# GpSimd as second choice for two kinds of low parts, w_in in four tensors, and the planner's new numbers

## The chip, the cores and the metric

The kernel runs on one core of a Trainium2 chip. The time is the device time of that core in microseconds (us). The engines are TensorE (PE in the profile; its weight loads PEld), VectorE (DVE), ScalarE (ACT), GpSimd (POOL) and SyncE (SP), whose queue issues nearly all DMAs. Three executions of the kernel before took 720.46, 721.92 and 986.96 us, median 721.92.

## The reference

Eight sequences b of 576 tokens go through an attention with 32 packed queries, twice, and then through a feed-forward layer with a gate:

```python
s = scale * q @ k.T ; a = exp(s - max) / (sum + 1e-9) ; sm_attn = a @ v
p_packed = sm_attn(p, k, v)             # 8 heads, 32 x 64 each
x = sm_attn(q, p_packed, p_packed)      # 576 x 512 for each b
h = x @ w_in                            # 512 -> 2048
g = h * erf(softplus(h))
out = g @ w_out                         # 2048 -> 512
```

w_in and w_out come as 64-bit floats. The kernel converts them to 32 bits itself, by a scaled copy on ACT and three bit operations on DVE.

## The kernel before, in words

Every product of the feed-forward layer is made from two 32-bit halves: a value is rounded to a high part (`hi`, type fp32r), the low part is the value minus that (`lo`), and PE multiplies hi by hi, lo by hi and hi by lo. So each tensor that PE reads there exists twice: `a2h` and `a2l` (the second attention's probabilities of a b), `wph` and `wpl` (w_in's block j multiplied into that b's packed values, "w prime"), `gh` and `gl` (the gated h), `woh` and `wol` (a tile of w_out).

The work is cut into units (b, f): f is one of 16 column tiles of 128 of the hidden 2048. `h_unit` makes h for one unit in two chunks of 288 tokens, six matmuls of 128x288 each, into two PSUM banks tagged `ps_h`, from which ACT copies them to `hs`. `gate_group` takes up to four units: ACT does softplus and erf (two tables, loaded each time), DVE multiplies (`hs<-t,hs`), rounds (`gh<-hs`) and subtracts (`gl<-hs,gh`). `o_unit` multiplies four token blocks by w_out's tile, three matmuls of 128x512 each, and adds them up in four PSUM banks. The 64 tokens of a b that are left over go through a DRAM tensor `rest` and are done for pairs of b (`o_rest`, matmuls `or`).

`load_w_in` and `load_w_out` bring a weight tile by DMA to a staging buffer (`wi`, `wos`), and `convert` turns it into 32 bits: ACT copy, DVE shift (`TENSOR_SCALAR`), and two DVE `SCALAR_TENSOR_TENSOR` that merge in the sign and the low word. w_out's tile is then rounded to `woh` (ACT or DVE) and `wol` is subtracted on DVE. The first block of w_in is loaded in two pairs (`load_w_in_pair`), staged in the room that blocks 2 and 3 take later.

What runs when is set by a list scheduler inside the kernel. Each operation is an `Op` with an engine, a key (its place in line, from the table `PLAN`), a cost in us and its dependencies. `Program.order` plays the program through with these costs: whenever an engine is free, it takes the ready operation with the lowest key whose buffers have room. The instructions are emitted in the order of the starts that come out, and each engine then runs its own in exactly that order. An operation may have a second engine (`also`): it stands in that engine's line too, with its key raised by a number from `PLAN["also"]`, and whichever of the two gets to it first has it.

Before the first h, PE waits for the first b's attention; `warm` transposes fill that time. Lines of the profile: L292 all matmuls, L297 to L301 the conversion, L346 wol, L457 the exponentials of the first two b, L549 and L550 a2h and a2l, L571 and L572 wph and wpl in one piece, L576 and L577 in two, L588 softplus, L593 erf, L598, L600 and L602 the gate's multiply, gh and gl, L624 the copy of h.

Of the kernel before, what the change touches and what calls it, by code (L numbers as in the profile page):

```python
# [43 lines left out]
    "first conv": (-9.39, 1.51),  # L44
    "whole k": 1,
}
# [24 lines left out]
class Program:  # L71
# [34 lines left out]
    def order(self):  # L106
# [14 lines left out]
        came = {op: 0.0 for op in self.ops}  # L121
# [11 lines left out]
        while events:  # L133
# [15 lines left out]
            for engine, line in ready.items():  # L149
# [3 lines left out]
                for i, (_, _, op) in enumerate(line):  # L153
# [10 lines left out]
                    break  # L164
                if pick is None:
                    continue
                op = line.pop(pick)[2]
# [21 lines left out]
                if engine in ("SP", "POOL") or op.kind == "dma":  # L189
                    state["bus"] = max(state["bus"], now + busy + self.SEND[0]) + op.dur / self.SEND[1]  # L190
                    end = state["bus"] + self.SEND[2] + PLAN["late"]
                else:
                    end = now + busy + op.dur
                count += 1
# [12 lines left out]
def act_us(n):  # L207
    return 0.05 + 0.00088 * n

# [6 lines left out]
def tile_pack_attention_moe(ctx: ExitStack, tc: tile.TileContext, qT, kT, v, pT, w_in, w_out, out, rest):  # L216
# [65 lines left out]
    def dma(key, size, emit, w, r, engine="SP", after=()):  # L282
        return prog.add(engine, key, 0.45 if engine != "POOL" else 1.0, size, lambda: line(engine, emit()), w, r,
                        kind="dma" if engine == "ACT" else 0, after=after)

    ident = fixed([P, P], "ident")
    w_in_sb = fixed([P, 4, DFF], "w_in_sb")
# [6 lines left out]
    def convert(key, dst, of, low, high, n, w, r):  # L294
# [3 lines left out]
        dve(key, n, lambda: nc.vector.tensor_scalar(bits(), bits(), 3, None, op0=ALU.logical_shift_left), w, (), True)  # L298
# [22 lines left out]
    def load_w_in_pair(sent, key, c):  # L321
        w = ((w_in_sb, (c, 0)), (w_in_sb, (c + 1, 0)))
        dst = lambda: w_in_sb[:, c:c + 2, 0:FB]
        src = w_in[c * P:(c + 2) * P, 0:FB].rearrange("(c p) n -> p c n", p=P)
        if w_in.dtype == F32:
            dma(sent, 2 * P * FB * 4, lambda: nc.sync.dma_start(dst(), src), w, ())
            return
        there = tuple((w_in_sb, (c + i, j)) for i in range(2) for j in (2, 3))
        raw = lambda: w_in_sb[:, c:c + 2, 2 * FB:4 * FB]
        dma(sent, 2 * P * FB * 8, lambda: nc.sync.dma_start(raw().bitcast(I64), src), there, ())  # L330
# [3 lines left out]
        convert(key, dst, None, words(0), words(1), 2 * FB, w, there)  # L334

    def load_w_in(sent, key, j, c):
        load_f32(sent, key, lambda: w_in_sb[:, c, j * FB:(j + 1) * FB], ((w_in_sb, (c, j)),),
                 w_in[c * P:(c + 1) * P, j * FB:(j + 1) * FB], f"wi{j}_{c}")

    def load_w_out(sent, key, f):  # L340
# [5 lines left out]
        dve(key, DM, lambda: nc.vector.tensor_tensor(lo[:], made[:], hi[:], op=ALU.subtract), (lo,), (made, hi))  # L346
# [3 lines left out]
    settled = []  # L350
# [11 lines left out]
    def products(key, names, wheres, left, rights, r, after=()):  # L362
# [12 lines left out]
        return places  # L375

    def attention(b, keys):
# [52 lines left out]
        if first:  # L430
# [4 lines left out]
                          [[pb] + [half(k, c, x) for c in range(NC)] for x in range(2)], () if roomy else settled[-1:])  # L435
# [78 lines left out]
        pt[b] = ptt  # L514
        ta, tb = big("ta", [P, 2, S]), big("tb", [P, 2, S])
        hi, lo = buf("a2h", [P, 2, S], f"a2h{b}", F32R), buf("a2l", [P, 2, S], f"a2l{b}", F32R)
        nb = 2 * HT // NK
        both = buf("mx", [P, 2 * nb], f"mx{b}")
# [35 lines left out]

    def w_prime(key, *pieces):
# [5 lines left out]

        def emit(b, j, hi, lo, banks, w, whole):
            return [mm(banks[r]()[NK * c:NK * c + NK, :], pt[b][64 * r:64 * r + 64, NK * c:NK * c + NK],
                       w_in_sb[64 * r:64 * r + 64, c, j * FB:(j + 1) * FB], start=True, stop=True)
                    for c in range(NC) for r in range(2)]
        pe(key, W_US * len(made), lambda: [i for piece in made for i in emit(*piece)], sum((x[5] for x in made), ()),
           [x for b, j in pieces for x in [pt[b]] + [(w_in_sb, (c, j)) for c in range(NC)]], 1)
        for i, (b, j, hi, lo, banks, w, whole) in reversed(list(enumerate(made))):
# [10 lines left out]
            wp[b, j] = (hi, lo)  # L579

    gs, group, before, sent_rest, heads = {}, [], [[]], {}, []

    def gate_group(e):
# [12 lines left out]
        for t, (hs, b, f, n) in zip(ts, group):  # L596
# [5 lines left out]
            dve(key, S, lambda hs=hs, ghi=ghi, glo=glo: nc.vector.tensor_tensor(glo[:], hs[:], ghi[:], op=ALU.subtract),  # L602
                (glo,), (hs, ghi))
# [6 lines left out]
    def h_unit(n, b, f):  # L610
# [3 lines left out]
        fo = f % PER * P  # L614
        for c in range(2):
            ps = buf("ps_h", [P, 512], f"h{b}_{f}_{c}")
            terms = [(r, w, a) for r in range(2) for w, a in ((whi, ahi), (whi, alo), (wlo, ahi))]
            cols = (lambda a, r, c=c: a[:, c, r * HT:(r + 1) * HT])
            if n == 0:
                terms = terms[0::3] + terms[1::3] + terms[2::3]  # L620
            made = pe(n + c / 2, 0.797, lambda c=c, ps=ps, terms=terms, cols=cols: [
                mm(ps[:, 0:HT], w[:, r, fo:fo + P], cols(a, r), start=(m == 0), stop=(m == 5))
                for m, (r, w, a) in enumerate(terms)], (ps,), (whi, wlo, (ahi, c), (alo, c)))
            op = act(n + c / 2 - PLAN["copy"], HT, lambda c=c, ps=ps: nc.scalar.copy(hs[:, c * HT:(c + 1) * HT], ps[:, 0:HT]),  # L624
                     ((hs, c),), (ps,))
            also("h", op, "DVE", dve_us(HT), lambda c=c, ps=ps: nc.vector.tensor_copy(hs[:, c * HT:(c + 1) * HT], ps[:, 0:HT]))
# [73 lines left out]
    w_prime(-40 + PLAN["wp first"], (0, 0))  # L700
# [87 lines left out]
```

## Time and profile before

| what | value |
|---|---|
| median of three executions | 721.92 us |
| the profiled execution's own time | 722.06 us |
| its span | 720.3 us |
| so outside the span | 1.8 us |
| PE busy | 705.3 us, 98% of the span |
| ACT busy | 495.8 us, 69% |
| DVE busy | 432.6 us, 60% |
| POOL busy | 7.9 us, 1% |
| first h matmul starts | 33.95 us |
| last o matmul starts | 710.92 us |

"Busy" counts the time in which at least one instruction of an engine is under way; overlapping matmuls count once. An idle time has behind it in brackets what ended it. Rows of a timeline give start, duration, engine, line, operation, output and inputs; the durations of consecutive instructions overlap by some 0.08 us on DVE and ACT, so what one more instruction costs is the distance from its start to the next start.

### The profile page before, as it was taken

How to read it: one execution, taken by the hardware profiler on the slowest of the kernel's cores; microseconds unless marked ns; L12 is line 12 of the kernel's file. 1: busy time of each engine (PE TensorE's matmuls, PEld its weight loads, DVE VectorE, ACT ScalarE, POOL GpSimd, SP SyncE). 2: the span in 40 equal slices, each digit the busy share in tenths (PEclk: the TensorE clock that was granted, in tenths of full speed). 3: DMA queues.
4: the chain of work that ended last, by engine and by line, in shares of the span. 5: the costliest groups of instructions: out<-in, count | busy, mean ns of one | idle time of the engine just before them, and what ended most of it. 6: DMA issues, size and time to landing. Idle time of an engine off the chain costs nothing.

```text
span 720.3 us, 13230 instructions
## 1 busy us (share of the span) xinstructions
PE 705.3 (98%) x5159; PEld 576.7 (80%) x5159; DVE 432.6 (60%) x707; ACT 495.8 (69%) x831; POOL 7.9 (1%) x14
## 2 busy tenths in 40 slices
PE   7889999999999999999999999999999999999997
PEld 6657887878878888787888878887878878788885
DVE  3899998898654754566545545467545564354540
ACT  3399999988874576766855758567858555676731
POOL 0000000002001000000000000000000000000000
PEclk9999999999999999999999999999999999999999
DMA  9962485754338300253006220063102210021104
GB/s 321 303 228 65 119 248 148 254 190 75 95 100 183 86 12 17 91 163 101 18 13 216 70 75 15 16 215 97 43 17 87 95 31 16 15 74 45 44 19 132
DMA packets 66399, 74.80 MB, mean 104 GB/s; under 512 B 40224, under 2 KB 42272, under 8 KB 66336
## 3 DMA queue, kind: packets, MB, share of 16 engines
q1 hardware_dynamic: 64816, 71.14, 32.0%
q0 software_dynamic: 1152, 2.10, 2.2%
q8 instruction: 40, 0.66, 0.4%
q10 hardware_dynamic: 368, 0.72, 0.3%
q14 instruction: 23, 0.19, 0.1%
HBM read 54.00 MB, written 19.92 MB: 103 GB/s over the span
## 4 chain that ended last, share of the span: by engine, by line
PE 83%; ACT 11%; DMA 3%; SPq 1%; issue 1%; DVE 0%; ACTq 0%
PE o L292 45%; PE h L292 25%; PE or L292 6%; PE wp L292 4%; PE s L292 2%; ACT L593 1%; ACT t L593 1%; ACT L588 1%; ACT hs L624 1%; ACT t L588 1%; DMA v<-v 1%; PE p L292 1%; DMA q<-qT 1%; DMA wi<-w_in 1%; PE t L477 1%; ACT w_in_sb L297 1%
## 5 line engine op out<-in xcount | busy, mean ns | idle before, releaser
L292 PE MATMUL o<-woh,gh 128*128 128x512 f32 x512 | 205.7, 402 | 0.5 <-DVE gh L600 0.5
L292 PE MATMUL o<-woh,gl 128*128 128x512 f32 x512 | 201.8, 394 | 0.5 <-DVE gl L602 0.5
L292 PE MATMUL o<-wol,gh 128*128 128x512 f32 x512 | 200.8, 392 | 0.0
L624 ACT COPY hs<-h 128x288 f32<-128x288 f32 x256 | 98.9, 395 | 129.9 <-PE h L292 128.9
L292 PE MATMUL h<-a2h,wph 128*128 128x288 f32 x512 | 152.5, 298 | 1.8 <-ACT a2h L549 1.6
L292 PE MATMUL h<-a2h,wpl 128*128 128x288 f32 x512 | 150.4, 294 | 0.7 <-DVE wpl L572 0.7
L292 PE MATMUL h<-a2l,wph 128*128 128x288 f32 x512 | 150.7, 295 | 0.3 <-DVE a2l L550 0.3
L598 DVE TENSOR_TENSOR hs<-t,hs 128x576 f32<-128x576 f32 x128 | 95.2, 753 | 60.0 <-ACT t L593 58.2
L292 PEld LDWEIGHTS o<-woh,gh 128*128 128x128 f32 x512 | 96.1, 188 | 34.1 <-issue 17.9
L292 PEld LDWEIGHTS o<-wol,gh 128*128 128x128 f32 x512 | 96.2, 188 | 22.0
L292 PEld LDWEIGHTS h<-a2h,wph 128*128 128x128 f32 x512 | 96.0, 188 | 14.9 <-ACT hs L624 3.6
L292 PEld LDWEIGHTS o<-woh,gl 128*128 128x128 f32 x512 | 96.2, 188 | 12.5 <-DVE gl L602 0.8
L600 DVE CAST gh<-hs 128x576 fp32r<-128x576 f32 x128 | 58.0, 456 | 77.6 <-PE o L292 76.1
L292 PEld LDWEIGHTS h<-a2l,wph 128*128 128x128 f32 x512 | 96.1, 188 | 8.8 <-DVE a2l L550 0.5
L602 DVE TENSOR_TENSOR gl<-hs,gh 128x576 fp32r<-128x576 f32 x128 | 96.1, 753 | 2.8 <-DMA rest<-gl 0.8
L292 PEld LDWEIGHTS h<-a2h,wpl 128*128 128x128 f32 x512 | 96.1, 188 | 0.9 <-DVE wpl L572 0.9
L588 ACT ACTIVATE t<-hs 128x576 f32<-128x576 f32 x128 | 87.2, 686 | 2.7 <-DVE hs L598 0.2
L593 ACT ACTIVATE t<-t 128x576 f32<-128x576 f32 x128 | 83.6, 685 | 0.4
L588 ACT ACT_TABLE_LOAD x38 | 48.8, 1283 | 0.7
L593 ACT ACT_TABLE_LOAD x38 | 48.8, 1283 | 0.7
L292 PE MATMUL or<-woh,g 128*128 128x512 f32 x128 | 40.2, 395 | 0.0
L654 ACT COPY ob<-o 128x512 f32<-128x512 f32 x40 | 22.8, 587 | 24.8 <-PE o L292 24.7
(98 smaller groups left out, 578.0 us busy)
## 6 DMA issues: line engine op xcount, KB each, us to landing
q<-qT SPq DMA_DIRECT2D x32, 288.0 KB, 4.2
v<-v SPq DMA_DIRECT2D x32, 256.0 KB, 3.8
wos<-w_out SPq DMA_DIRECT2D x16, 512.0 KB, 3.5
out<-ob SPq DMA_DIRECT2D x32, 256.0 KB, 2.8
g<-rest SPq DMA_DIRECT2D x16, 512.0 KB, 3.2
k<-kT SPq DMA_DIRECT2D x26, 288.0 KB, 4.5
wi<-w_in SPq DMA_DIRECT2D x12, 512.0 KB, 4.9
rest<-gh SPq DMA_DIRECT2D x128, 32.0 KB, 1.5
```

Of the source, the lines that this page charges most:

```text
L292: return nc.tensor.matmul(*args, **kw)
L297: act(key, n * 1.06, lambda: nc.scalar.mul(dst(), high().bitcast(F32), F64_SCALE), w, r)
L477: return [nc.tensor.transpose(tbanks[x]()[:, (j % 2 * 2 + r) * P:(j % 2 * 2 + r + 1) * P], a[:, r, j * P:(j + 1) * P], ident[:]) for j in ...
L588: done.append(act(n + PLAN["lag"] - PLAN["act"] - 2, S, lambda t=t, hs=hs: nc.scalar.activation(t[:], hs[:], AF.Softplus), (t,), (hs,), ru ...
L593: erfs.append(act(e + PLAN["lag"] - PLAN["act"] - 4 + i, S, lambda t=t: nc.scalar.activation(t[:], t[:], AF.Erf), (t,), (), run="erf", kin ...
L598: dve(key, S, lambda t=t, hs=hs: nc.vector.tensor_tensor(hs[:], t[:], hs[:], op=ALU.mult), (hs,), (t,))
L600: op = dve(key, S, lambda hs=hs, ghi=ghi: nc.vector.tensor_copy(ghi[:], hs[:]), (ghi,), (hs,), True)
L602: dve(key, S, lambda hs=hs, ghi=ghi, glo=glo: nc.vector.tensor_tensor(glo[:], hs[:], ghi[:], op=ALU.subtract), (glo,), (hs, ghi))
L624: op = act(n + c / 2 - PLAN["copy"], HT, lambda c=c, ps=ps: nc.scalar.copy(hs[:, c * HT:(c + 1) * HT], ps[:, 0:HT]), ((hs, c),), (ps,))
L654: act(key - 1, DM, lambda: nc.scalar.copy(ob[:], to[:]), (ob,), (to,))
```

## The change

**Second choices.** The subtraction that makes `wol` and the one that makes `gl` in the first 24 units (`"low until": 24`) get GpSimd as a second engine, both with nothing added to their key (`'w_out low': 0, 'low': 0`). The planner books `pool_us(n)`, 0.3 + 0.0037 n us, for them. A third possible second choice, the conversion's shift, is written but not in the table.

**w_in in four tensors.** One tensor of 128 x 4 x 2048 becomes four of 128 x 4 x 512, `w_in0` to `w_in3`. The first block's pairs are staged in the whole of `w_in2` and of `w_in3`.

**Other edits.** The first w prime is made by a function of its own, `w_prime_first`, which moves its two PSUM banks out one by one (512 columns each) where one instruction moved both (1024). Options that are switched off come along: `direct` and the branches that need it, `patience` (0), `halves` (1). The key of "packs" changes from 2.35 to 4.61, and "norm", which nothing used, goes.

```diff
-    "also": {'w_out': 10.23, 'turned': 8.26, 'packs': 2.35, 'norm': 0.2},
+    "also": {'w_out': 10.23, 'turned': 8.26, 'packs': 4.61, 'w_out low': 0, 'low': 0},
...
+    "low until": 24,
...
+def pool_us(n):
+    return 0.3 + 0.0037 * n
...
-    w_in_sb = fixed([P, 4, DFF], "w_in_sb")
+    HALVES = PLAN["halves"]
+    FN = FB // HALVES
+    w0 = [fixed([P, NC, FN], f"w_in0{x}") for x in range(HALVES)]
+    wi = [None] + [fixed([P, NC, FB], f"w_in{j}") for j in range(1, NFB)]
...
-        dve(key, DM, lambda: nc.vector.tensor_tensor(lo[:], made[:], hi[:], op=ALU.subtract), (lo,), (made, hi))
+        op = dve(key, DM, lambda: nc.vector.tensor_tensor(lo[:], made[:], hi[:], op=ALU.subtract), (lo,), (made, hi))
+        also("w_out low", op, "POOL", pool_us(DM), lambda: nc.gpsimd.tensor_tensor(lo[:], made[:], hi[:], op=ALU.subtract))
...
+            for r in range(2):
+                act(keys[x], FN, lambda hi=hi, r=r, banks=banks, at=at: nc.scalar.copy(hi[:, r, at], banks[r]()[:, 0:FN]),
+                    ((hi, (x, r)),), (w[r % len(w)],))
...
+            if n < PLAN["low until"]:
+                also("low", op, "POOL", pool_us(S), lambda hs=hs, ghi=ghi, glo=glo: nc.gpsimd.tensor_tensor(
+                    glo[:], hs[:], ghi[:], op=ALU.subtract))
...
-    w_prime(-40 + PLAN["wp first"], (0, 0))
+    w_prime_first([-40 + k for k in PLAN["wp first"]])
```

What the scheduler makes of it is seen in the order of the instructions on each engine. POOL had nothing between its start and its eight output DMAs. It now has 24 subtractions there, six `wol` and 18 `gl`. These are the first of them (in a name such as gl_3_934, 3 is the tile f, and the last number tells instances apart):

```order
L374 TENSOR_TENSOR wol_722<-wo_672,woh_718 128x512
L722 TENSOR_TENSOR gl_1_786<-hs_1_566,gh_1_780 128x576
L374 TENSOR_TENSOR wol_867<-wo_727,woh_852 128x512
L374 TENSOR_TENSOR wol_890<-wo_764,woh_869 128x512
L722 TENSOR_TENSOR gl_3_934<-hs_3_599,gh_3_927 128x576
L722 TENSOR_TENSOR gl_4_998<-hs_4_807,gh_4_986 128x576
L722 TENSOR_TENSOR gl_5_1086<-hs_5_849,gh_5_1074 128x576
L722 TENSOR_TENSOR gl_6_1115<-hs_6_881,gh_6_1112 128x576
L722 TENSOR_TENSOR gl_7_1151<-hs_7_929,gh_7_1141 128x576
```

Eight of these nine stand ahead of the last gate rounding of the first segment (gh_7) or beside it: three wol and five gl, up to gl_6.

On ACT, around the first a2h, before (wi_0 to wi_3 are the four pieces of w_in's second block, a_1 the second b's exponentials, hs the copied h):

```order
L297 ACTIVATE w_in_sb<-wi_0_232 128x512
L297 ACTIVATE w_in_sb<-wi_1_239 128x512
L549 CAST a2h_503<-tb_491 128x576
L297 ACTIVATE w_in_sb<-wi_2_247 128x512
L549 CAST a2h_503<-tb_491 128x576
L457 ACTIVATE a_1_535,ms_441<-s_1_0_0_391,m_522 128x288
L457 ACTIVATE a_1_535,ms_441<-s_1_0_1_393,m_522 128x288
L457 ACTIVATE a_1_535,ms_441<-s_1_1_0_402,m_522 128x288
L457 ACTIVATE a_1_535,ms_441<-s_1_1_1_404,m_522 128x288
```

And there now:

```order
L320 ACTIVATE w_in_84<-wi_0_235 128x512
L320 ACTIVATE w_in_84<-wi_1_242 128x512
L594 CAST a2h_504<-tb_491 128x576
L320 ACTIVATE w_in_84<-wi_2_250 128x512
L320 ACTIVATE w_in_84<-wi_3_257 128x512
L751 COPY hs_0_538<-h_0_0_520 128x288
L499 ACTIVATE a_1_548,ms_440<-s_1_0_0_395,m_512 128x288
L499 ACTIVATE a_1_548,ms_440<-s_1_0_1_397,m_512 128x288
L499 ACTIVATE a_1_548,ms_440<-s_1_1_0_407,m_512 128x288
L499 ACTIVATE a_1_548,ms_440<-s_1_1_1_409,m_512 128x288
L594 CAST a2h_504<-tb_491 128x576
```

The fourth piece wi_3 and a copy of h have moved ahead of the exponentials, and the second a2h behind them.

Further on, on ACT ahead of the second w prime's high part, before:

```order
L588 ACTIVATE t_1_691<-hs_1_553 128x576
L297 ACTIVATE wo_722<-wos_668 128x512
L593 ACT_TABLE_LOAD
L593 ACTIVATE t_1_691<-t_1_691 128x576
L588 ACT_TABLE_LOAD
L588 ACTIVATE t_2_758<-hs_2_645 128x576
L571 CAST wph_1_771<-wp_1_749 128x1024
L297 ACTIVATE wo_774<-wos_715 128x512
```

And there now:

```order
L705 ACTIVATE t_1_694<-hs_1_566 128x576
L320 ACTIVATE wo_727<-wos_661 128x512
L710 ACT_TABLE_LOAD
L710 ACTIVATE t_1_694<-t_1_694 128x576
L320 ACTIVATE wo_764<-wos_716 128x512
L705 ACT_TABLE_LOAD
L705 ACTIVATE t_2_766<-hs_2_574 128x576
L668 CAST wph_1_778<-wp_1_753 128x1024
```

One more conversion of a w_out tile (wo_764) stands ahead of wph_1.

On DVE, between the first gl and the second w prime's low part, before:

```order
L346 TENSOR_TENSOR wol_747<-wo_656,woh_717 128x512
L538 TENSOR_REDUCE mx_760<-ta_726 128x36
L598 TENSOR_TENSOR hs_1_553<-t_1_691,hs_1_553 128x576
L539 TENSOR_TENSOR ta_726<-ta_726,mx_760 128x1152
L572 TENSOR_TENSOR wpl_1_776<-wp_1_749,wph_1_771 128x1024
L600 CAST gh_1_781<-hs_1_553 128x576
L298 TENSOR_SCALAR wo_722<-wo_722 128x512
L602 TENSOR_TENSOR gl_1_792<-hs_1_553,gh_1_781 128x576
```

And there now:

```order
L321 TENSOR_SCALAR wo_727<-wo_727 128x512
L583 TENSOR_REDUCE mx_762<-ta_731 128x36
L715 TENSOR_TENSOR hs_1_566<-t_1_694,hs_1_566 128x576
L584 TENSOR_TENSOR ta_731<-ta_731,mx_762 128x1152
L717 CAST gh_1_780<-hs_1_566 128x576
L669 TENSOR_TENSOR wpl_1_784<-wp_1_753,wph_1_778 128x1024
L323 SCALAR_TENSOR_TENSOR wo_727<-wos_661,wo_727 128x512
```

wol and gl_1 are gone from DVE here, and the shift and gh_1 have moved ahead of wpl_1. PE's instructions are the same in number, and their last 80 rows are in the same order; in the first part of the program h and o blocks have changed places by a few.

More of the change, by code (lines that the diff above doesn't have):

```diff
@@ L120, in order @@
         state = {"table": None, "within": False, "kind": 0, "bus": 0.0}
-        came = {op: 0.0 for op in self.ops}
+        unsent, due = {op: len(op.deps) for op in self.ops}, {op: 0.0 for op in self.ops}
+        soon = {e: [] for e in ready}
+        patience, until = PLAN["patience"]
         events, count = [(0.0, 0, None)], 0
@@ L164, in order @@
                     break
+                soon[engine] = [(t, op) for t, op in soon[engine] if waits[op]]
                 if pick is None:
                     continue
-                op = line.pop(pick)[2]
+                op = line[pick][2]
+                if now < until and any(op2.key < op.key - 2 and t - now < patience and now + op.busy > t + 0.05
+                                       for t, op2 in soon[engine]):
+                    continue
+                line.pop(pick)
                 if op.other:
@@ L188, in order @@
                 free[engine] = now + busy
[L189 removed]
+                if op.kind == "dma":
                     state["bus"] = max(state["bus"], now + busy + self.SEND[0]) + op.dur / self.SEND[1]
@@ L193, in order @@
                     end = now + busy + op.dur
+                for nxt in then[op]:
+                    unsent[nxt] -= 1
+                    due[nxt] = max(due[nxt], end)
+                    if not unsent[nxt]:
+                        soon[nxt.engine].append((due[nxt], nxt))
                 count += 1
@@ L560, in w_prime, with piece @@
             made.append((b, j, hi, lo, *banks_of(f"wp{b}_{j}", where)))
+        def piece(j):
+            return [(w0[x], slice(x * FN, (x + 1) * FN)) for x in range(HALVES)] if j == 0 else [(wi[j], slice(0, FB))]
         def emit(b, j, hi, lo, banks, w, whole):
[L563 to L567, printed above, removed]
+            return [mm(banks[r]()[NK * c:NK * c + NK, at], pt[b][64 * r:64 * r + 64, NK * c:NK * c + NK],
+                       t[64 * r:64 * r + 64, c, :], start=True, stop=True)
+                    for t, at in piece(j) for c in range(NC) for r in range(2)]
+        pe(key, W_US * len(made), lambda: [i for m in made for i in emit(*m)], sum((x[5] for x in made), ()),
+           [x for b, j in pieces for x in [pt[b]] + [(t, c) for t, _ in piece(j) for c in range(NC)]], 1)
         for i, (b, j, hi, lo, banks, w, whole) in reversed(list(enumerate(made))):
@@ L614, in h_unit @@
         fo = f % PER * P
+        if (b, f // PER) == (0, 0):
+            x = fo // FN
+            needs = [(t, (x, r)) for t in (whi, wlo) for r in range(2)]
+        else:
+            needs = [whi, wlo]
         for c in range(2):
```

142 lines of the change are left out of this document (113 added, 29 removed).

## The prediction

> **What bounds the kernel now.** I read the page's first part, then the busy times by stretch, then who waited for whom on PE, then the timeline from 31 to 57 us, engine by engine.
>
> ```profile
> span 720.3 us, 13230 instructions
> PE 705.3 (98%) x5159; PEld 576.7 (80%) x5159; DVE 432.6 (60%) x707; ACT 495.8 (69%) x831; POOL 7.9 (1%) x14
> ```
>
> ```profile
> 20.00:40.00 20.00, 17.01 (x185) 13.83 (x185) 16.75 (x40) 9.76 (x22) 0.00 (x0) 1.00 0.95 319
> 40.00:60.00 20.00, 17.49 (x205) 10.99 (x204) 19.47 (x34) 19.80 (x28) 0.00 (x0) 0.91 0.41 137
> 60.00:80.00 20.00, 19.95 (x125) 16.42 (x124) 19.21 (x31) 19.89 (x34) 0.00 (x0) 1.00 0.31 93
> 80.00:100.00 20.00, 20.00 (x138) 16.91 (x137) 19.23 (x34) 19.10 (x35) 0.00 (x0) 1.00 0.64 199
> ...
> 250.00:300.00 50.00, 50.00 (x331) 41.02 (x332) 23.88 (x40) 34.34 (x58) 0.00 (x0) 1.00 0.07 15
> ```
>
> In each row the first number behind the stretch and its length is PE's busy time, then PEld, DVE, ACT and POOL, then the granted clock. From 60 us on PE has no gap worth naming, at clock 1.00: the rest of the run is as long as PE's matmuls. DVE and ACT are full from 40 to 100 us (19.47 and 19.80 of 20, and so on) and half idle later, so only up to about 100 us can relief on DVE, which is what the change brings, mean anything at all. What it can win there is PE's waiting:
>
> ```profile
> PE h L292 <- ACT a2h L549: 1.6, 1, 1.6
> ...
> PE h L292 <- DVE wpl L572: 0.7, 1, 0.7
> PE o L292 <- DVE gl L602: 0.5, 1, 0.5
> PE o L292 <- DVE gh L600: 0.5, 1, 0.5
> ...
> PE s L292 <- ACT hs L624: 0.4, 1, 0.4
> ```
>
> The 1.6 us is the first h. Its time is set here:
>
> ```profile
> 31.37 0.69 ACT L297 ACTIVATE w_in_sb<-wi 128x512 f32<-128x512 f32 x1 [3.57 <-DMA wi<-w_in]
> 32.68 0.66 ACT L297 ACTIVATE w_in_sb<-wi 128x512 f32<-128x512 f32 x1 [0.62 <-DMA wi<-w_in]
> 33.24 0.66 ACT L549 CAST a2h<-tb 128x576 fp32r<-128x576 f32 x1
> 33.95 0.53 PE L292 MATMUL h<-a2h,wph 128*128 128x288 f32 x2 [1.64 <-ACT a2h L549]
> 33.93 0.76 DVE L550 TENSOR_TENSOR a2l<-tb,a2h 128x576 fp32r<-128x576 f32 x1 [1.68 <-ACT a2h L549]
> ```
>
> ACT runs in order, and a2h stands behind the second piece of w_in, whose DMA lands at 32.65. DVE idles 1.68 us for a2h. The last place where PE waits is the second block's h; its wpl comes from DVE:
>
> ```profile
> 54.72 1.23 DVE L572 TENSOR_TENSOR wpl<-wp,wph 128x1024 fp32r<-128x1024 f32 x1
> ...
> 56.00 0.40 PE L292 MATMUL h<-a2h,wpl 128*128 128x288 f32 x1 [0.67 <-DVE wpl L572]
> ```
>
> Behind 56 us the trace names no wait of PE before its tail, so what this wpl loses or gains, the end does.
>
> **The change, part by part.**
>
> *The first h stays.* ACT's order has the same two pieces ahead of the first a2h, and the queue's first 54 rows bring the same transfers. The new `w_prime_first` splits a copy and a subtraction in two and moves the softmax's DVE steps about; all that lies ahead of DVE's 1.68 us of idle time and behind a DMA, so it costs nothing. Without that cover it would cost one more start, 0.1 to 0.2 us. h starts at 33.95 again.
>
> *w_in in four tensors: nothing.* No row of PE's waits names w_in, the shapes and bytes per partition are the same, and the staging still ends with the first block's conversion.
>
> *ACT's new order, which is a loss.* Two steps. First, the fourth piece of w_in now stands ahead of the second b's exponentials:
>
> ```profile
> L315 SPq DMA_DIRECT2D wi<-w_in x4: 430/430/584, 25.1 to 26.6; - x4
> ...
> DMA to landing us min/median/max: 6.3/7.4/9.2
> ```
>
> ```profile
> 35.98 1.49 ACT a L457 x6
> ```
>
> The fourth is issued at 26.6; I give it the longest flight, 9.2, since flights grow in a queue that is full: it lands at 35.8. Its conversion (0.57 start to start, 32.68 to 33.24) ends the wait at 36.4, a copy of h adds 0.3, and the exponentials start at 36.7 and not at 35.98: 0.7 late. Second, from there to wph the list of ACT gains a2h (0.6) and one conversion of w_out (0.57) and loses the w_in piece (0.57) and one copy of h (0.3): 0.3 more. The stretch has no room:
>
> ```profile
> 47.26 1.28 ACT L588 ACT_TABLE_LOAD   x1
> ...
> 53.10 0.69 ACT L588 ACTIVATE t<-hs 128x576 f32<-128x576 f32 x1
> 53.69 1.00 ACT L571 CAST wph<-wp 128x1024 fp32r<-128x1024 f32 x1
> ```
>
> ACT idles 0.2 us between 40 and 60 us, so of 0.7 + 0.3, 0.8 reach wph: it ends at 54.69 + 0.8 = 55.5. DVE loses wol there (0.60) and gains a shift and gh_1 (0.34 + 0.36): it would be ready at 54.72 + 0.1 = 54.8 and now waits for ACT, so wpl starts at 55.5 and not at 54.72. PE's h goes on 0.8 us later: **+0.8**. The gl wait earlier (0.5) may shrink or grow by as much without a trace, since PE comes to this later wait anyhow.
>
> *Subtractions moved to POOL.* What a moved one saves DVE, and what the same thing may cost POOL:
>
> ```profile
> 88.70 0.76 DVE L602 TENSOR_TENSOR gl<-hs,gh 128x576 fp32r<-128x576 f32 x1
> 89.38 0.69 DVE L346 TENSOR_TENSOR wol<-wo,woh 128x512 fp32r<-128x512 f32 x1
> 89.98 0.42 DVE L298 TENSOR_SCALAR w_in_sb<-w_in_sb 128x512 uint32<-128x512 uint32 x1
> ...
> 90.75 0.40 PE L292 MATMUL o<-woh,gl 128*128 128x512 f32 x1
> ```
>
> ```profile
> masks.py:199 POOL TENSOR_SCALAR_AFFINE_SELECT ident<-ident 128x128 f32<-128x128 f32 x1 | 0.3, 289 | 0.1
> masks.py:197 POOL MEMSET ident<- 128x128 f32 x1 | 0.2, 206 | 0.3 <-POOLq L779 0.3
> ...
> L779 POOL MEMSET const-float32-0.0<- 128x1 f32 x1 | 0.1, 99 | 0.2 <-issue 0.2
> ```
>
> gl frees 0.68 and wol 0.60 of DVE. POOL has no such operation in this trace. From below: the memset's slope, (206 - 99) / 127 = 0.84 ns an element, gives 0.58 us for 576. From above: the select's, (289 - 99) / 128 = 1.48 ns with one input, doubled for two inputs, 1.8 us; the planner's booking of 2.43 is a number of the code, and I keep it for the far end. I take 1.4, nearest to the select, which also computes. That POOL's own time is longer than DVE's is covered: the first gl that moves, gl_1, ends at 57.3 before and is used at 59.78, 2.5 us later, and even 2.43 us of POOL from gh's end at 56.3 would be there in time.
>
> ```profile
> 56.57 0.75 DVE L602 TENSOR_TENSOR gl<-hs,gh 128x576 fp32r<-128x576 f32 x1
> ...
> 59.78 0.40 PE L292 MATMUL o<-woh,gl 128*128 128x512 f32 x1
> ```
>
> The question is what an operation on POOL does to DVE beside it: from nothing to holding it for the whole 1.4 us. Up to gh_7 eight are moved, 3 x 0.60 + 5 x 0.68 = 5.2 us of DVE. At half of 1.4 each they take 5.6 back; DVE is 0.4 late, and the last gl of that segment has 90.75 - 89.46 = 1.3 us of room (rows above). So in the likeliest case relief and hold cancel: **0**. Should the cover of 1.3 be gone, it costs the 0.4.
>
> The Trainium skill's "SBUF — State Buffer", section "Who interferes with whom", says that VectorE and GpSimd share one port pair, and that a VectorE instruction with two SBUF inputs and a GpSimd instruction that reads SBUF shut each other out entirely, for the length of the one that came first. By that rule the sum would be that of the second rival below, 727.5; no row of this trace has the two side by side. "GPSIMD Engine Reference", section 3.1, of the Trainium skill gives 4.497 us for a two-input add of 2048 elements; an estimate from it for 576 is 1.3 us.
>
> **Sum.** The profiled execution took 722.06 us, 1.8 of it outside the span, and lies 0.14 over the median 721.92. 722.06 + 0 + 0 + 0.8 + 0 = **722.9**.
>
> **The rivals.**
>
> *Relief wins.* ACT catches up (wi_3 lands before 35, so the exponentials aren't late), and DVE's freed time lets gl and wpl come earlier: PE's waits for gh, gl, wpl and hs go, 0.5 + 0.5 + 0.7 + 0.4 = 2.1 us, to 720.0. For it: all four are DVE or ACT work in a full stretch. Against it: only one subtraction of those moved stands ahead of that wpl, and wph's ACT chain got longer, not shorter.
>
> *POOL holds DVE.* Each of the eight keeps DVE standing for 1.4 us: 11.2 - 5.2 = 6.0 late by the last gl, less 1.3 of room: 4.7 on PE, with ACT's 0.8: 727.5. It decides as soon as a moved operation takes more than (5.2 + 1.3) / 8 = 0.8 us from DVE. For it: DVE's instructions in that stretch nearly all read two SBUF tensors, as POOL's do, and DVE is 96% busy, so nearly every POOL operation meets one. Against it: transposes, reductions and PSUM inputs lie between. At 2.43 us the same sum is 19.4 - 5.2 - 1.3 = 12.9, 735.8, and eight more follow up to the second segment's end, so that 2% (14.4 us) can be passed.
>
> *Nothing moves.* The order ends in the same time, 722.1. It lies inside the first case's range.
>
> **How the numbers follow.** The likeliest case, 721.8 to 724.5, gets 0.50: ACT's 0.8 stands between 0 and 1.6 (wi_3 a little earlier or later), and the hold between 0 and 0.9 us. Relief wins: 0.17, 719.5 to 721.8. POOL holds DVE: 0.24, 724.5 to 730. The same at more than 1.6 us each: 0.09, above 730, half of it above 736.4. The range from 719.5 to 729.5 leaves out some 0.12. About 2% is what a measurement of this kernel can tell from no change, 707.5 to 736.4. Faster than that isn't to be had, since the first h hangs on a DMA and PE is full from 60 us on: 0.01. Slower: 0.05. Same: 0.94.
>
> **What would show it.** First h at 33.9 to 34.0, behind a2h. The exponentials of the second b at 36.7, ACT waiting for wi just before. The second block's wpl starting 0.8 later than 54.72, with ACT's wph as what ended DVE's wait. POOL with 24 TENSOR_TENSOR of 1.0 to 1.8 us, and DVE's gh and hs rows still 0.45 and 0.75 us; if they are stretched, or DVE's idle time is ended by POOL, the hold is real, and PE will show waits for gl with POOL as the engine. It would be wrong if PE shows new waits between 60 and 130 us, or if h starts before 33.

## The result, and the profile after

The changed kernel takes **730.55 us** (median of 728.90 to 731.26), the kernel before 721.19 in the same comparison: a ratio of **1.0132, 95% interval 1.0103 to 1.0160**. It is 9.4 us slower, 1 us beyond the upper end of the range on record. One execution of the kernel before is far off the others (986.96 us) and is left out of the ratio. The profiled execution of the changed kernel took 728.9 us and is the fastest of its four, so the spans of the two profiles differ by 6.8 us only; causes are read from the profiles, sizes from the medians.

The page's first part for the kernel after:

```profile
span 727.1 us, 13259 instructions
PE 708.0 (97%) x5157; PEld 576.6 (79%) x5157; DVE 440.9 (61%) x688; ACT 495.4 (68%) x828; POOL 49.0 (7%) x38
```

DVE has 19 instructions fewer and is busy 8.3 us *longer* (432.6 before). PE has two instructions fewer, both `warm` transposes, so its number isn't quite the same. PE's busy time grew by 2.7 us, the span by 6.8: more than half of the loss is PE standing still. The busy times by stretch of the kernel after (us; then PE, PEld, DVE, ACT, POOL, then the clock) show where:

```profile
40.00:60.00 20.00, 16.66 (x199) 10.36 (x198) 19.71 (x33) 19.77 (x28) 2.83 (x2) 0.91 0.44 134
60.00:80.00 20.00, 18.78 (x115) 16.01 (x121) 19.90 (x26) 18.39 (x31) 7.65 (x4) 1.00 0.34 101
80.00:100.00 20.00, 19.43 (x125) 15.21 (x110) 19.87 (x26) 18.34 (x32) 8.54 (x5) 1.00 0.42 123
100.00:150.00 50.00, 49.34 (x411) 37.95 (x403) 44.98 (x72) 43.12 (x74) 15.64 (x9) 1.00 0.65 201
150.00:200.00 50.00, 48.19 (x310) 39.40 (x309) 39.60 (x58) 41.08 (x70) 10.15 (x9) 1.00 0.47 127
250.00:300.00 50.00, 50.00 (x315) 41.02 (x314) 25.35 (x45) 30.41 (x52) 0.00 (x0) 1.00 0.17 41
```

Against the rows of before, PE lacks 0.8 us in 40:60, 1.2 in 60:80 and 0.6 in 80:100, and it isn't full at 100:200 either; at 250 us it is. The stretches with gaps are those in which POOL works. PE's waits in the kernel after (engine, matmul, what it waited for: us in total, times, longest):

```profile
PE o L315 <- DVE gl L719: 2.4, 2, 1.3
PE h L315 <- DVE wpl L669: 2.2, 3, 1.2
...
PE o L315 <- POOL gl L722: 0.5, 1, 0.5
PE o L315 <- DVE gh L717: 0.5, 1, 0.5
...
PE h L315 <- ACT a2h L594: 0.3, 1, 0.3
```

gl on DVE was 0.5 before and is 2.4, wpl was 0.7 and is 2.2. POOL itself is waited for once, 0.5 us. So in this kernel the moved subtractions are hardly ever late themselves; what stayed on DVE is. The groups of the kernel after (busy us, mean ns of one), DVE's with those of the kernel before in the fence behind:

```profile
L715 DVE TENSOR_TENSOR hs<-t,hs 128x576 f32<-128x576 f32 x128 | 102.4, 811 | 60.0 <-ACT t L710 58.0
...
L722 POOL TENSOR_TENSOR gl<-hs,gh 128x576 fp32r<-128x576 f32 x18 | 31.6, 1756 | 64.3 <-DVE gh L717 44.0 <-issue 9.0 <-ACT t L705 6.4
L374 POOL TENSOR_TENSOR wol<-wo,woh 128x512 fp32r<-128x512 f32 x6 | 9.5, 1588 | 65.3 <-DVE woh L372 46.8 <-ACT woh L371 18.4
```

```profile
L598 DVE TENSOR_TENSOR hs<-t,hs 128x576 f32<-128x576 f32 x128 | 95.2, 753 | 60.0 <-ACT t L593 58.2
```

The same 128 products of hs became 58 ns longer on average, 7.2 us in all, and they weren't edited. One such product in the timeline of the kernel after, DVE and then POOL:

```profile
82.06 0.42 DVE L321 TENSOR_SCALAR wo<-wo 128x512 uint32<-128x512 uint32 x1
82.40 2.00 DVE L715 TENSOR_TENSOR hs<-t,hs 128x576 f32<-128x576 f32 x1
...
82.22 1.55 POOL L722 TENSOR_TENSOR gl<-hs,gh 128x576 fp32r<-128x576 f32 x1 [4.94 <-DVE gh L717]
```

POOL's gl begins at 82.22, while the shift is under way; hs begins on DVE at 82.40 and takes 2.00 us and not 0.76. It is held for 1.24 us and ends 0.62 after POOL has ended (83.77), a little less than its own length. Where the held instruction is one for which PE waits, PE pays at once. The first moved subtraction, in the same timeline, DVE, POOL, PE:

```profile
47.24 0.45 DVE L717 CAST gh<-hs 128x576 fp32r<-128x576 f32 x1
47.73 1.71 DVE L719 TENSOR_TENSOR gl<-hs,gh 128x576 fp32r<-128x576 f32 x1
...
47.41 1.42 POOL L374 TENSOR_TENSOR wol<-wo,woh 128x512 fp32r<-128x512 f32 x1 [46.10 <-DVE woh L372]
...
49.49 0.50 PE L315 MATMUL o<-woh,gl 128*128 128x512 f32 x1 [1.25 <-DVE gl L719]
```

wol on POOL starts 0.3 us ahead of DVE's gl; gl takes 1.71 and PE waits 1.25 for it, 0.5 before.

### The profile page after: what moved, and what is told of

Read it like the earlier page. It is cut to its first block, busy times and chain, and to the rows that moved or that the text cites. A ratio compares the mean times of both kernels' runs of the same rounds, so it can differ in the third digit from the quotient of the medians.

```text
span 727.1 us, 13259 instructions
## 1 busy us (share of the span) xinstructions
PE 708.0 (97%) x5157; PEld 576.6 (79%) x5157; DVE 440.9 (61%) x688; ACT 495.4 (68%) x828; POOL 49.0 (7%) x38
## 4 chain that ended last, share of the span: by engine, by line
PE 81%; DVE 9%; DMA 4%; ACT 2%; issue 2%; SPq 1%; DVEq 0%; ACTq 0%
PE o L315 44%; PE h L315 24%; PE or L315 6%; PE wp L315 3%; DVE hs L715 2%; DMA v<-v 2%; PE s L315 2%; PE p L315 1%; DMA wi<-w_in 1%; DMA q<-qT 1%; DVE gh L717 1%; DVE wpl L669 1%; DVE w_in L323 1%; PE t L519 1%; DVE wo L323 1%
## 5 line engine op out<-in xcount | busy, mean ns | idle before, releaser
L715 DVE TENSOR_TENSOR hs<-t,hs 128x576 f32<-128x576 f32 x128 | 102.4, 811 | 60.0 <-ACT t L710 58.0
L717 DVE CAST gh<-hs 128x576 fp32r<-128x576 f32 x128 | 60.9, 479 | 78.2 <-PE o L315 76.7
L719 DVE TENSOR_TENSOR gl<-hs,gh 128x576 fp32r<-128x576 f32 x110 | 83.4, 762 | 2.0
L781 ACT COPY ob<-o 128x512 f32<-128x512 f32 x40 | 22.5, 587 | 24.7 <-PE o L315 24.4
```

The lines of the kernel that those rows point to most:

```text
L715: dve(key, S, lambda t=t, hs=hs: nc.vector.tensor_tensor(hs[:], t[:], hs[:], op=ALU.mult), (hs,), (t,))
L717: op = dve(key, S, lambda hs=hs, ghi=ghi: nc.vector.tensor_copy(ghi[:], hs[:]), (ghi,), (hs,), True)
L719: op = dve(key, S, lambda hs=hs, ghi=ghi, glo=glo: nc.vector.tensor_tensor(glo[:], hs[:], ghi[:], op=ALU.subtract), (glo,), (hs, ghi))
L781: act(key - 1, DM, lambda: nc.scalar.copy(ob[:], to[:]), (ob,), (to,))
```

## The experiments

Two theories stood at the start. *Theory A*: the subtractions on POOL hold DVE. *Theory B*: the other order, and the other edits, cost it. All ratios are to the kernel before on the same chip.

**The same order, the subtractions back on DVE.** The changed kernel's plan is kept; what it books on POOL is issued to DVE at the same place of the list.

```diff
-            op.other = (engine, PLAN["also"][what], busy, lambda: line(engine, emit()))
+            on = "DVE" if engine == "POOL" else engine
+            op.other = (engine, PLAN["also"][what], busy, lambda: line(on, emit()))
...
-        also("w_out low", op, "POOL", pool_us(DM), lambda: nc.gpsimd.tensor_tensor(lo[:], made[:], hi[:], op=ALU.subtract))
+        also("w_out low", op, "POOL", pool_us(DM), lambda: nc.vector.tensor_tensor(lo[:], made[:], hi[:], op=ALU.subtract))
```

> The changed kernel with its plan and its order untouched, but the 24 subtractions planned for GpSimd are issued to VectorE at the places where GpSimd would have started them. Theory A, an operation on GpSimd holds VectorE's instruction beside it: the 24 holds (24 us of stretched VectorE rows in the changed kernel) go and 24 x 0.66 = 16 us of VectorE work come back, 8 us less in all; the time goes back to 720 to 724, and no VectorE row is longer than in the kernel before. Rival B, the new order itself is bad (places too tight for gl and wol): PE waits at the same places, 727 to 731. Rival C, the other edits (four tensors for w_in, the first w prime in two pieces): 727 to 731 as well, told apart by the next kernel.

724.88 us, ratio 1.0050 (1.0035 to 1.0065). So in this order POOL's part is 1.0132 less 1.0050, 5.9 us, and 3.6 us of the loss come without any subtraction on POOL. A row of the page's first part, and one of PE's waits, of this kernel:

```profile
PE 707.4 (98%) x5157; PEld 577.3 (80%) x5157; DVE 433.9 (60%) x712; ACT 495.3 (68%) x828; POOL 7.9 (1%) x14
```

```profile
PE h L316 <- ACT wph L669: 1.4, 1, 1.4
```

The 24 subtractions on DVE make DVE 7.0 us *less* busy than on POOL. On DVE they are worth 18 x 0.68 + 6 x 0.60 = 15.8 us, so on POOL they took 22.8 from it, **0.95 us each**. The wait for wph stands where the prediction had its +0.8, but it doesn't measure ACT's new order: the run e11_round below, whose lists are those of the kernel before, shows 1.0 us for wph too, since PE came there earlier. What the new order costs is read from two points of PE's list, the first h and the second block's h with wpl. From one to the other PE takes 22.05 us in the kernel before (33.95 to 56.00), 23.59 in the kernel after (32.40 to 55.99) and 23.70 here (34.45 to 58.15): 1.5 to 1.6 us more, with POOL's subtractions or without.

**Without the second choices.** All other edits are kept, and the list is planned anew.

```diff
-    "also": {'w_out': 10.23, 'turned': 8.26, 'packs': 4.61, 'w_out low': 0, 'low': 0},
+    "also": {'w_out': 10.23, 'turned': 8.26, 'packs': 4.61},
```

> The changed kernel without the two second choices on GpSimd, everything else as changed, planned anew. Theory A: 719 to 723, as before. Rival B (the order): also 719 to 723, since it is planned anew. Rival C (the other edits cost the time): 727 to 731.

723.46 us, 1.0029 (1.0018 to 1.0040). The other edits, with the order that they bring, cost 2.1 us on their own, where the sum had 0 for the edits and 0.8 for ACT's row.

**The kernel before with the second choices alone.**

```diff
-    "also": {'w_out': 10.23, 'turned': 8.26, 'packs': 2.35, 'norm': 0.2},
+    "also": {'w_out': 10.23, 'turned': 8.26, 'packs': 2.35, 'norm': 0.2, 'w_out low': 0, 'low': 0},
+    "low until": 24,
...
+def pool_us(n):
+    return 0.3 + 0.0037 * n
```

> The kernel before with the two second choices on GpSimd alone, planned anew with the same booking; w_in in one tensor, the first w prime whole. Theory A: 726 to 732, with VectorE rows stretched by up to 1.24 us beside each GpSimd operation. Rival C: 720 to 723. Rival B would leave it open, since the order is another one.

729.35 us, 1.0116 (1.0099 to 1.0132): 8.4 us from this part alone, with 25 subtractions on POOL in a list planned anew.

**Each subtraction replaced by two memsets on POOL**, in the changed kernel's order; these low parts are zero, so the products lack them.

```diff
-                also("low", op, "POOL", pool_us(S), lambda hs=hs, ghi=ghi, glo=glo: nc.gpsimd.tensor_tensor(
-                    glo[:], hs[:], ghi[:], op=ALU.subtract))
+                also("low", op, "POOL", pool_us(S), lambda hs=hs, ghi=ghi, glo=glo: [
+                    line("POOL", nc.gpsimd.memset(glo[:].bitcast(F32), 0.0)) for _ in range(2)])
```

> The changed kernel with its plan and order, but each of the 24 subtractions on GpSimd is replaced by two memsets of the same tile to zero (so those low parts are left out, and the output is less exact): GpSimd is busy for 2 x 0.6 us at the same places, writes as much and reads nothing from SBUF. Theory A in the form that a GpSimd operation that reads SBUF excludes a VectorE operation with two SBUF inputs: TENSOR_TENSOR and SCALAR_TENSOR_TENSOR rows of VectorE keep 0.75 and 0.68 us beside it, and the time is 718 to 723; one-input CAST and TENSOR_SCALAR rows, which run at the doubled rate, may still be held. If any GpSimd operation of that length holds VectorE: 726 to 731. If it is not VectorE at all but GpSimd's own lateness: about 728, for the memsets are 0.4 us shorter than the 1.7 us of the subtractions.

724.72 us, 1.0044 (1.0029 to 1.0059): as with the subtractions on DVE, 3 us above the kernel before for the order's sake. From its page, the busy times and three groups:

```profile
PE 706.7 (98%) x5157; PEld 577.4 (80%) x5157; DVE 423.8 (59%) x688; ACT 494.6 (68%) x828; POOL 37.2 (5%) x62
...
L718 DVE TENSOR_TENSOR hs<-t,hs 128x576 f32<-128x576 f32 x128 | 95.1, 753 | 64.0 <-ACT t L713 62.0
...
L720 DVE CAST gh<-hs 128x576 fp32r<-128x576 f32 x128 | 60.4, 475 | 80.5 <-PE o L318 79.0
...
L726 POOL MEMSET gl<- 128x576 f32 x36 | 22.5, 626 | 131.6 <-PE o L318 130.6
```

hs is back at 753 ns. POOL was busy beside it all the same (22.5 us on gl), but it reads nothing. What holds DVE's two-input instructions is POOL's reading, not its being at work; gh's cast, with one input, is still a little longer (475 against 456 ns before). Eight of the 48 memsets run at the program's start, since they wait for no data; that limits the comparison to those that remain. For the same reason the run takes away the lateness of POOL's results together with the hold, so it shows that hs is no longer held, but doesn't price the hold alone. And DVE is 10.1 us less busy than with the subtractions on DVE (423.8 against 433.9), while the time is the same: in this order DVE's relief by itself brings nothing that the times show.

**A planner that knows the hold.** POOL's subtraction is booked at 0.3 + 0.0026 an element, near its real time, and 1.24 us on DVE beside it.

```diff
+                if engine == "POOL" and op.kind != "dma":
+                    free["DVE"] = max(free["DVE"], now) + HOLD
...
-    return 0.3 + 0.0037 * n
+    return 0.3 + 0.0026 * n
```

> The changed kernel, but the planner is told what the changed kernel's trace shows: a subtraction on GpSimd is booked at 0.3 + 0.0026 n us (1.8 us for 576), and it also moves VectorE's next start 1.24 us back in the plan. GpSimd still takes a subtraction whenever it is free. Theory A, the hold costs VectorE more than the moved work saves: an honest plan can only place things better, VectorE still loses some 0.4 us for each, and the time stays at 724 to 730, over the kernel without second choices (723.5). Rival B (only the plan's wrong booking hurt): 720 to 723.

732.55 us, 1.0168 (1.0145 to 1.0191): slower still, a clear miss of both cases expected. The list takes POOL 32 times and not 24, since its choice goes by the one earliest start and not by what the hold does to others, and PE waits in new places:

```profile
PE o L322 <- POOL gl L729: 2.8, 2, 2.0
PE h L322 <- DVE a2l L602: 1.9, 2, 1.6
PE wp L322 <- ACT a1t L531: 1.8, 1, 1.8
```

**The second choice for all 128 units.**

```diff
-    "low until": 24,
+    "low until": 128,
```

> The changed kernel with the second choice of gl on GpSimd for all 128 units and not the first 24 only. Theory A with its limit, the hold costs time only where VectorE is full, up to about 200 us: more subtractions go to GpSimd, VectorE's busy time rises by some 0.4 us for each of them, and the time stays within 2 us of the changed kernel (729 to 733). Rival: every hold costs PE, then each further one adds 0.3 us or more, 740 and over.

730.24 us, 1.0125 (1.0109 to 1.0141), the time of the changed kernel, with 58 subtractions on POOL and not 24. Its busy times by stretch:

```profile
300.00:400.00 100.00, 100.00 (x816) 82.19 (x815) 58.41 (x86) 71.11 (x121) 11.92 (x7) 1.00 0.32 97
```

Where DVE is 58% busy a hold costs PE nothing: 100.00 of 100.

**ACT's order at the first h.** In the kernel before, the second b's pieces of w_in are converted behind the first a2h; two of ACT's rows change places.

```diff
-        act(key, n * 1.06, lambda: nc.scalar.mul(dst(), high().bitcast(F32), F64_SCALE), w, r)
+        act(key, n * 1.06, lambda: nc.scalar.mul(dst(), high().bitcast(F32), F64_SCALE), w, r, after=after)
```

> The kernel before with one thing changed: ScalarE's conversion of the second, third and fourth piece of w_in's second block comes after the first a2h copy (the planner keeps all else, the order differs on ScalarE alone, by these two rows). The first h no longer waits for the second piece's DMA: it starts at about 32.0 and not at 33.95. If ScalarE's chain from there to the second w prime sets the end, as the kernel before's trace has it, the end comes 0.7 to 1.5 us earlier: 720.0 to 721.0. If the first h is hidden by the second b's chain: 721.4, no change.

721.15 us, 1.0001 (0.9991 to 1.0010): no change. In its profile h starts at 33.16, neither at the expected 32.0 nor at 33.95: a2h now waits for DVE's transposed probabilities (tb) and no longer for the w_in piece. PE stays some 0.8 us ahead of the profile of before to the end, but the medians are equal, so this lead isn't seen as a gain of the kernel's.

**The four tensors, the first w prime whole.** As the kernel without second choices, but the first w prime goes out in one piece as before.

```diff
-        if (b, f // PER) == (0, 0):
+        if False:
...
-    w_prime_first([-40 + k for k in PLAN["wp first"]])
+    w_prime(-40 + PLAN["wp first"][0], (0, 0))
```

> The changed kernel without second choices on GpSimd and with the first w prime moved out of PSUM whole, as before; w_in stays in four tensors. The order is that of the kernel before up to about 240 instructions of ScalarE. If the 2.0 us that the kernel without second choices is slower come from the order that the split of that copy brings about: 720.5 to 722. If they come from the four tensors: 723 to 724.

722.45 us, 1.0021 (1.0012 to 1.0030): 1.5 us that neither the split nor POOL explains. From the first h to the second block's h with wpl PE takes 22.15 us again, where the kernel without second choices takes 23.53: ACT's new order comes with the split. PE's list here is that of the kernel before up to some 190 us and another one behind, where PE loses 1.1 us. The cause is a number in the change's core: a chunk of h is booked at 0.06 + 0.00256 x 288 = 0.79728 us and no longer at 0.797. Put back,

```diff
-            made = pe(n + c / 2, 0.06 + 0.00256 * n1, lambda c=c, ps=ps, terms=terms, cols=cols, n1=n1: [
+            made = pe(n + c / 2, 0.797, lambda c=c, ps=ps, terms=terms, cols=cols, n1=n1: [
```

> The kernel before with w_in in four tensors, as in the run before this one (722.45, ratio 1.0021), but the planner's cost of a 288-column chunk of h is again the 0.797 us of the kernel before, not the 0.79728 that the change's formula gives. With it PE's and SP's rows are those of the kernel before throughout, and ACT's and DVE's too but for the shapes of w_in's conversions; with 0.79728 they part from 190 us on. Theory A (the 1.5 us of the run before come from the order that the 0.28 ns tips over, the four tensors cost nothing): 721.0, ratio 0.999 to 1.001. Theory B (the four tensors themselves cost it, by addresses or waits): 722.4, ratio 1.002.

721.26 us, **0.9995 (0.9986 to 1.0004)**. PE's and SP's lists are those of before again, row by row. So w_in in four tensors costs nothing, and 0.28 ns in a booking cost the 1.5 us by tipping the list. (In the changed kernel itself the same 0.28 ns moves no row.)

**Fewer second choices.** The kernel before with second choices, but for g only in the first 8 units: 15 subtractions and not 25.

```diff
-    "low until": 24,
+    "low until": 8,
```

> The kernel before with the second choices alone, the low parts of g for the first 8 units and not 24: 15 subtractions go to GpSimd (11 of w_out, 4 of g) and not 25. Theory A (each one holds DVE for about 1.0 us, saves it 0.6 to 0.7, and is paid on PE): the cost goes with the number, so 8.4 x 15 / 25 = 5.0 over before, 726.2, between 724.5 and 727.5; DVE's two-input operations are stretched by some 13 to 15 us in all. Theory B (the list's other order costs it, not the hold): either all of the 8.4 or nearly none of it, 729.5 or below 723.

727.63 us, 1.0088 (1.0070 to 1.0106): 6.4 us, a little above what theory A allowed. DVE is busy 3.0 us longer, far too little for 6.4. One row of PE's waits is new, and the kernel with 25 subtractions has it too; behind it stand two rows of the timeline, DVE and ACT:

```profile
PE o L297 <- ACT ob L663: 2.2, 1, 2.2
```

```profile
89.45 1.67 DVE L304 SCALAR_TENSOR_TENSOR w_in_sb<-wi,w_in_sb 128x512 uint32<-128x512 uint32 x1
...
95.42 0.67 ACT L302 ACTIVATE w_in_sb<-wi 128x512 f32<-128x512 f32 x1 [0.61 <-DMA wi<-w_in]
```

ACT has this conversion of w_in (at 95.42), a table load (96.11) and a softplus (97.40) ahead of the copy of ob (98.27), for which PE waits. Most of that is order. But the conversion waits 0.61 for its DMA, which is issued at 91.91 after a wait for DVE's work on an earlier piece, and DVE was held in that work for 1.0 us (1.67 and not 0.68). So a hold can reach PE by way of a DMA as well. Neither theory is enough alone, and the last two runs take order out altogether.

**The same 24 subtractions on POOL, in the order of before.** The kernel before keeps its plan and its list row by row; the 24 that the changed kernel moved are issued to POOL.

```diff
+        if f in (1, 2, 3, 13, 14, 15):
+            op.emit = lambda: line("POOL", nc.gpsimd.tensor_tensor(lo[:], made[:], hi[:], op=ALU.subtract))
...
+            if n in (1, 3, 4, 5, 6, 7, 8, 9, 10, 11, 12, 13, 15, 16, 17, 18, 19, 22):
+                op.emit = lambda hs=hs, ghi=ghi, glo=glo: line("POOL", nc.gpsimd.tensor_tensor(
+                    glo[:], hs[:], ghi[:], op=ALU.subtract))
```

> The kernel before with its plan and its order kept row by row on every engine; only the instructions of the same 24 subtractions (18 of g, 6 of w_out) are issued to GpSimd and not to DVE, so DVE's list is the old one without these 24 rows. Theory A (the hold costs the time): GpSimd's subtractions stretch DVE by about 24 us again and free 15.8; the same 24 in the changed kernel's own order made 1.0132 out of 1.005, so here 1.008 over before: 727.2, between 726 and 728.5. Theory B (the list's other order costs most, the subtractions on GpSimd little): below 724.

724.78 us, 1.0045 (1.0031 to 1.0059): **3.2 us**, between the two theories and outside both. DVE is 437.4 us busy, 4.8 more than before with 15.8 us of work fewer: 20.6 over 24, 0.86 us a hold. PE's rows are the same as before, one by one, so its delay can be followed. It comes in steps, among them 0.3 us each for a wol and a gl that POOL itself delivers late, 0.3 for a wol that DVE makes late at 91 us, and 1.4 in the w prime at 108 us, behind DVE's sm. Its timeline at two places, POOL and DVE:

```profile
48.36 1.72 POOL L348 TENSOR_TENSOR wol<-wo,woh 128x512 fp32r<-128x512 f32 x1 [47.05 <-DVE woh L345]
...
81.26 1.82 POOL L607 TENSOR_TENSOR gl<-hs,gh 128x576 fp32r<-128x576 f32 x1 [2.73 <-DVE gh L602]
...
48.19 0.75 DVE L604 TENSOR_TENSOR gl<-hs,gh 128x576 fp32r<-128x576 f32 x1
48.86 1.57 DVE L528 STREAM_TRANSPOSE ta<-s 128x288 f32<-128x288 f32 x4
...
81.69 1.67 DVE L298 TENSOR_SCALAR wo<-wo 128x512 uint32<-128x512 uint32 x1
```

At 81.69 a shift is held, 1.67 us and not 0.42, and the hold is again 1.25. At 48 us the same wol meets the same gl as in the kernel after, but gl was issued 0.17 us earlier than wol: it keeps its 0.75, wol waits for it, and the transposes behind it aren't held (1.57 for four, 1.56 before). Which of the two comes first decides whether PE waits 0.5 us or 1.25.

**Only the first nine of them.**

```diff
-        if f in (1, 2, 3, 13, 14, 15):
+        if f in (1, 2, 3):
...
-            if n in (1, 3, 4, 5, 6, 7, 8, 9, 10, 11, 12, 13, 15, 16, 17, 18, 19, 22):
+            if n in (1, 3, 4, 5, 6, 7):
```

> As the run beside it, but only the first nine are issued to GpSimd (3 of w_out, 6 of g, those that run up to the first segment's end), the other 15 stay on DVE. By the size measured for a hold (1.0 us) nine take 9.0 and free 3 x 0.60 + 6 x 0.68 = 5.9: 3.1 more on DVE, less the 1.3 of room at the segment's last gl, 1.8 on PE: 723.2. If the place of a hold decides and not the sum (a held gl or wpl for which PE waits costs PE at once what DVE wins back later), more: 724 to 726. If the second segment's holds cost most of it: below 722.5.

723.38 us, 1.0026 (1.0014 to 1.0038), 1.9 us, the 1.8 that were expected from the size of a hold. DVE is busy 434.9 us, 2.3 more for 5.9 fewer of work: 0.91 us a hold.

**Where PE loses it.** The table below is worked out from the traces: how much later than in the kernel before PE starts its h and o, at equal PE work done since the first h (us; minus is earlier). The times are those of the kernel before. The profiled execution of the first row was that kernel's fastest, those of the second and the last row their kernels' slowest, so the rows are compared within themselves.

```
                                first h   59 us   89 us  109 us  177 us    end
after                             -1.54   -0.12   +2.13   +4.73   +6.78  +6.54
its order, all on DVE             +0.50   +3.57   +3.16   +3.95   +3.97  +3.74
order of before, 24 on POOL       -0.49   -0.47   +0.52   +3.20   +2.57  +2.73
order of before, first 9 on POOL  -0.06   +0.05   +1.06   +2.15   +3.21  +3.21
```

In the changed kernel's order PE loses 1.4 us (after) to 3.1 us (all on DVE) between the first h and 59 us; behind that the order alone costs 0.2. With POOL's subtractions it costs 6.7 behind 59 us, and the same subtractions in the old order cost 3.2.

## Why the prediction was wrong

**The first h: not fixed.** It was put at 33.95 "again". In the kernel after ACT and PE show, in the timeline:

```profile
31.69 0.66 ACT L594 CAST a2h<-tb 128x576 fp32r<-128x576 f32 x1
...
32.40 0.53 PE L315 MATMUL h<-a2h,wph 128*128 128x288 f32 x2 [0.25 <-ACT a2h L594]
```

1.55 us earlier, since the w_in piece landed earlier. Over all profiles it begins between 32.3 and 34.6, and between 33.06 and 34.19 where the lists ahead of it are the same. The cover of DVE's 1.68 us of idle time isn't fixed either: in five of the profiles, one of them with the lists of before (the first nine), a2h waits 1.1 to 1.7 us for DVE's tb; in these five PE also waited for a k by 1.2 to 1.5 us. The early start may make up a part of the difference between the 6.8 us of the two profiles and the 9.4 of the medians. In this profile the lead was gone by 59 us (-0.12).

**Four tensors: nothing. Right**, shown at 0.9995. **The split of the first w prime: nothing. Not right, by way of the list.** Without second choices the kernel loses 2.1 us; with the first w prime whole and the old booking of h, nothing. The split is what brings ACT's new order (23.53 us and 22.15 between the two points above). A time of its own isn't measured: with and without it the ratios are 1.0029 and 1.0021, and their intervals overlap.

**ACT's new order, +0.8: a loss, as forecast, but 1.5 to 1.6 us.** It is hidden in the profile of the kernel after by the early first h: wph begins at 53.63 there and at 53.69 before, and wpl at 54.72 in both. The first of the two steps was put down to the wrong cause. The fourth piece of w_in was there by 33.67 and not at 35.8; the exponentials begin 2.86 us behind the first h and not 2.04, and wait for DVE:

```profile
35.26 0.50 ACT L499 ACTIVATE a<-s,m 128x288 f32<-128x288 f32 x1 [0.62 <-DVE tb L593]
...
55.99 0.40 PE L315 MATMUL h<-a2h,wpl 128*128 128x288 f32 x1 [0.62 <-DVE wpl L669]
```

From the exponentials to wph ACT takes 18.37 us, 17.71 before: 0.7 for the second step, where 0.3 was reckoned. All of this is far less than the 9.4.

**POOL: 0. This is the step that failed**: "At half of 1.4 each they take 5.6 back", so that "relief and hold cancel". Three things were mis-sized.

- *A hold.* It was taken as 0.7 and measured as 0.86 to 0.95 averaged over all, 1.24 for each full meeting. The price of POOL's own operation was right: its row takes 1.41 us for 576 elements where nothing holds it (at 54.95, below), 1.4 taken. Half of it was the wrong share: measured against the same rows without POOL, 18 of the 24 subtractions in the kernel after hold a DVE instruction for 0.95 to 1.24 us, the other six for less or not at all. The point given, 0.8 us, was passed. The rival named the case: it was given 0.24.
- *How many count.* Eight were counted, up to the first segment's last gl, against 1.3 us of room. The table shows further loss between 89 and 177 us (+4.65), and the first nine alone cost 1.9 of the 3.2 in the old order. The harm doesn't end with the first segment: the last of the 24 starts at 170.7 us. The 34 more that the run with all 128 units has, all of them behind that, add nothing to the time.
- *What the list makes of it.* The sum gave the new order ACT's 0.8 and took the holds as independent of it. The measured parts are, by ratios: POOL's subtractions in the old order 0.45%, the new order without POOL 0.50%, both together 1.32%. The remaining 0.37%, 2.7 us, belongs to the two at once; with the three intervals it lies between next to nothing and 0.7%, so its size is only roughly known. The reading is that the new list puts DVE's work where it believes DVE free, and the holds fall on a gl or a wpl for which PE waits.

Why the new list puts the holds worse is shown at one place (47 us, above), and argued for the rest. Of the 3.6 us of the new order without POOL, 1.5 to 1.6 are located (the stretch up to the second block's h); where the rest comes from is open. A booking with the real hold didn't mend it.

**The rivals.** *Relief wins* was excluded: no kernel with a subtraction on POOL was faster, nor was the one with memsets, where DVE had the relief and hs wasn't held. *POOL holds DVE*, 727.5 with a range of 724.5 to 730, had the mechanism. The time lies just above its range, in that of the case with more than 1.6 us a hold, which no hold took. That 727.5 comes nearest of the sums is in part luck: its 4.7 us for eight holds are too many (nine cost 1.9 in the old order), and it lacked the holds behind the eighth and the order's own 3.6 us in place of 0.8. The Trainium skill's "SBUF — State Buffer", section "Who interferes with whom", gave this rule, an exclusive lock for the whole instruction between GpSimd's reads and VectorE's second input or doubled rate. The traces agree as far as they show it: hs, with two inputs, is held for 1.24 us; a DVE instruction issued first goes undisturbed (gl at 48.19: 0.75 us); memsets that read nothing leave hs at 753 ns; and a subtraction with one input in PSUM isn't held, as these rows of the kernel after show, DVE and POOL:

```profile
54.72 1.21 DVE L669 TENSOR_TENSOR wpl<-wp,wph 128x1024 fp32r<-128x1024 f32 x1
...
54.95 1.41 POOL L722 TENSOR_TENSOR gl<-hs,gh 128x576 fp32r<-128x576 f32 x1 [6.12 <-DVE gh L717]
```

This rival should have been the forecast: the reasons set against it (transposes, reductions and PSUM inputs lie between) concern the instructions that a POOL operation passes, but the operation needs to meet only one other, and 18 of the 24 did. Six were spared in part or whole, where a wpl, a transpose or a reduction came first.

**What would show it.** Of the signs named for the forecast, the first h at 33.9, the exponentials at 36.7 behind a wait for wi, and a later wpl did not come. Those named for the hold did: hs and gh are stretched (811 against 753 ns, 479 against 456), and PE has new waits between 60 and 130 us, though for DVE's gl and wpl and only once for POOL. POOL's 24 rows last 1.3 to 2.4 us, where 1.0 to 1.8 were expected.

## What to carry to other kernels

In this kernel work taken from VectorE to GpSimd was no relief: 0.65 us of it cost 0.9 us of hold. Only where VectorE had 40% idle time was that free, and an instruction such as wpl, with an input in PSUM, kept its time beside GpSimd. Ask of such a move what VectorE will start next, not only what it gives away. To price such a move, first issue the moved instructions to the other engine in the unchanged order, then the unchanged instructions in the new order: here the two parts, 3.2 and 3.6 us, came to less than the whole of 9.4. And where a list scheduler sets the order, any number in its bookings is an edit of its own, 0.28 ns included.

## What the runs showed of the chip

- A full hold is regular: 1.24 us by a subtraction of 576 elements on whichever DVE instruction of that kind is next (hs 0.76 to 2.00, a shift 0.42 to 1.67). From the end of the shift for which POOL waited (82.48) to POOL's own end (83.77) are 1.29 us.
- The profile shows the hold as *busy* time of DVE, not as a wait. DVE's waits and idle times don't name POOL; it is seen in the single rows and in the changed mean of an unchanged group (753 to 811 ns).
- GpSimd's subtraction takes longer in the rows than it works: a mean of 1756 ns for 576 elements, where the row beside wpl takes 1.41 us. The rest is its own wait for the DVE instruction under way; the longest row, 2.42 us at 69.51, spans 1.1 us of a2l on DVE.
- The first h starts between 32.3 and 34.6 us over all profiles, and between 33.06 and 34.19 in five with the same lists up to there. It follows the later of two things, the landing of a w_in piece or DVE's tb. Executions of one kernel differ by about 2 us in most runs, and a single profile's start shouldn't be read as a kernel's.
